# Attention and two gated layers on one core: the first chunk's first group multiplied in float32, its weights and activations split later

## Chip, core and metric

The kernel runs on one core of one Trainium2 chip. The metric is the device time of one execution in microseconds (us). TensorE (PE) multiplies into PSUM banks, VectorE (DVE) and ScalarE (ACT) do the elementwise work, GpSimd (POOL) helps, and SyncE (SP) issues every transfer from one queue, in order.

## What is computed

Three layers stand one behind the other. Attention over 2 x 8 heads, 768 positions and 64 features sees 31 neighbours and one summary (maximum of k, mean of v) of each of 24 blocks of 32 rows; its output is 1536 tokens x 512. A gated layer of width 1536 and a leaky one of width 2048 follow:

```python
x = attention(q, k, v)                     # 1536 x 512, float32
y = (x @ w_a * (x @ w_b)) @ w_out          # moe_*, weights are float64
h = y @ w_in;  out = maximum(0.01 * h, h) @ w2_out   # moe2_*, float64
```

## The kernel before

The tokens are worked in three chunks of 512 (`NC`), the feature axis in pieces of 128. Attention handles one *pair* at a time: two heads and 512 query rows; four pairs make a chunk. A pair runs through k and q transposes (L472, L500), scores (L518), masked minimum and exponential (L531, L535), scaling (L543 to L545), transposes of the probabilities (L553) and the value product (L565). Block sums of v enter through `v_sums` (POOL additions L425, DVE reduction L435), `v_place` (L452) and `put_sums` (POOL copy L196), once for each half of the heads.

The weights come as float64, in 512 KB pieces: `stage` loads one, and `convert` makes a float32 number of its two words in five steps (L332 and L336, L340, L345, L351, L357) and then splits it into a rounded float32r part (`high`, ACT, L362) and what is left (`rest_of`, DVE, L365). The activations are split in the same way (L575 and L576 for x, L603 and L604 for the gated product). A product is three float32r matmuls of 128x512 (`mm3`, L583): part by part, without the product of the two small parts.

The gated layer is worked in three groups (`s`) of `M1` = 4 slices of its width, and in each group chunk by chunk; a unit is a group and a chunk. In a unit four slices give a and b (4 x 2 x 4 products), then the four output tiles of y take 16 more. The first two slices of unit (0, 0) are multiplied during attention of chunk 0, as each x tile comes (`early`). Attention of chunk 1 is interleaved with unit (0, 0), that of chunk 2 with unit (0, 1). A group's 12 converted pieces serve all three chunks, and 14 fit (`W_EARLY`).

Order: the code emits instructions by due times (`attention_ops`), background steps of `convert` go in between (`tick`), and a scheduler then fixes one order for each engine at build time. At run time every engine, and SP's queue, goes strictly in that order and waits for what it needs.

Of the kernel before, what the change touches and what calls it, by code (L numbers as in the profile page):

```python
# [21 lines left out]
def kernel(  # L22
# [43 lines left out]
    M1 = 4  # L66
# [13 lines left out]
    q_p = att.enter_context(tc.tile_pool(name="q", bufs=3))  # L80
# [113 lines left out]
    def put_sums(i, p):  # L194
        for j, b, hp, g, n in runs(p):
            nc.gpsimd.tensor_copy(  # L196
                out=vw_of[i][W : W + NB, :, j * G : (j + n) * G, :],
                in_=vs_t[b, 2 * hp // HV][:, 2 * hp % HV : 2 * hp % HV + 2, :]
                .unsqueeze(2)
                .to_broadcast([NB, 2, n * G, D]),  # L200
            )
# [5 lines left out]
    def attention_ops():  # L207
# [3 lines left out]
        for i, p in enumerate(sum(pairs, [])):  # L211
# [4 lines left out]
            for m, (b, hp) in enumerate(dict.fromkeys(x[:2] for x in p)):  # L216
                vi, r = divmod(2 * hp, HV)
                if (b, hp) not in seen:
                    seen.add((b, hp))
                    add(-18, LOAD, load_k, b, hp)  # L220
                    for j in range(2):
                        add(2 * m + j - 12, PRODUCT, k_prep, b, hp, j)
                    if r == 0:
                        add(-4, LOAD, load_vb, b, vi)
                        add(-4, SIDE, v_sums, b, vi)
                        add(7, PRODUCT, v_place, b, vi)
            add(-14, LOAD, load_q, i, p)
# [15 lines left out]
    for t in vw_t:  # L243
        nc.gpsimd.memset(t, 0.0)
# [4 lines left out]
    ident = const.tile([P, P], F32, tag="ident", name="ident")  # L249
    make_identity(nc, ident)  # L250
    negm = []
    for kind in ("first", "mid", "last"):
        t = const.tile([P, P], F32, tag=f"negm_{kind}", name=f"negm_{kind}")
        nc.gpsimd.memset(t, 0.0)
        nc.gpsimd.memset(t[:, W : W + NB], -math.log(BLK))
        nc.gpsimd.memset(t[:, W + NB : SC], BIG)
        for c in range(2):
            for o, c0, c1 in ((0, 0, W), (W, SC, P)):
                loc = t[c * W : (c + 1) * W, c0:c1]

                nc.gpsimd.affine_select(
                    out=loc, in_=loc, compare_op=ALU.is_ge, fill=BIG,
                    base=o - 1, pattern=[[1, c1 - c0]], channel_multiplier=-1,
                )
                nc.gpsimd.affine_select(
                    out=loc, in_=loc, compare_op=ALU.is_ge, fill=BIG,
                    base=2 * WIN - 1 - o, pattern=[[-1, c1 - c0]], channel_multiplier=1,
                )
        if kind == "first":
            nc.gpsimd.memset(t[:, 0:WIN], BIG)  # L270
        if kind == "last":
            nc.gpsimd.memset(t[:, P - WIN :], BIG)
        negm.append(t)
# [4 lines left out]
    units = [(s, c) for s in range(NF1 // M1) for c in range(NC)]  # L278
    slices2 = [(s * M2 + i, c) for s in range(NF2 // M2) for c in range(NC) for i in range(M2)]
    uses = []  # L280
    for s, c in units:
        fs = range(s * M1, (s + 1) * M1)
        uses += [(nm, f) for f in fs for nm in "ab"] + [("o", f) for f in fs]
# [11 lines left out]
    room = {"early": W_EARLY, "late": 0}  # L295
# [20 lines left out]
    def convert():  # L316
# [8 lines left out]
        home = "early" if room["early"] else "late"  # L325
        assert room[home], key
        room[home] -= 1
        t = {}

        def low():  # L330
            t["r"] = wcv_p.tile([P, 512], I32, tag="wr", name="wr")
# [3 lines left out]
            t["c"] = wcv_p.tile([P, 512], I32, tag="wc", name="wc")  # L335
# [23 lines left out]
        def high():  # L359
            pool = wsp_p if home == "early" else late["wsp"]  # L360
            t["w"] = pool.tile([P, 2, 512], F32R, tag="wsp", name="wsp")
            nc.scalar.copy(out=t["w"][:, 0], in_=t["c"].bitcast(F32))  # L362

        def rest_of():
            nc.vector.tensor_tensor(  # L365
                out=t["w"][:, 1], in0=t["c"].bitcast(F32), in1=t["w"][:, 0].bitcast(F32),
                op=ALU.subtract,
            )
            w_of[key] = t["w"], home

        bg.extend([low, clamp, shift, join, add, high, rest_of])

    def may_convert():
        return cnt["conv"] < len(pieces) and room["early"] + room["late"] > 0

    def tick(n):
        for _ in range(n):
            if not bg and may_convert():
                convert()
# [9 lines left out]
    def weights(key):  # L389
# [443 lines left out]
```

## Time and profile before

| | us |
|---|---|
| median of 3 runs (661.61 to 661.86) | 661.84 |
| profiled execution | 661.53 |
| its span | 659.8 |
| PE busy in the span | 636.2 (96%) |
| DVE, ACT, POOL busy | 418.1, 270.8, 48.5 |
| mean granted PE clock (1 is 2.4 GHz) | 0.992 |

"Busy" counts an instruction from start to end, and matmuls overlap; so where throughput matters, a matmul is priced by the distance from one start to the next in a dense run, and not by its mean duration. The page puts 88% of the chain that ended last on PE. Its slices show where that is not so: PE below 9 tenths only in the first 100 us, and there DVE at 9 tenths and the transfers at 200 GB/s.

### The profile page before, as it was taken

How to read it: one execution, taken by the hardware profiler on the slowest of the kernel's cores; microseconds unless marked ns; L12 is line 12 of the kernel's file. 1: busy time of each engine (PE TensorE's matmuls, PEld its weight loads, DVE VectorE, ACT ScalarE, POOL GpSimd, SP SyncE). 2: the span in 40 equal slices, each digit the busy share in tenths (PEclk: the TensorE clock that was granted, in tenths of full speed). 3: DMA queues.
4: the chain of work that ended last, by engine and by line, in shares of the span. 5: the costliest groups of instructions: out<-in, count | busy, mean ns of one | idle time of the engine just before them, and what ended most of it. 6: DMA issues, size and time to landing. Idle time of an engine off the chain costs nothing.

```text
span 659.8 us, 9339 instructions
## 1 busy us (share of the span) xinstructions
PE 636.2 (96%) x3440; PEld 519.3 (79%) x3440; DVE 418.1 (63%) x952; ACT 270.8 (41%) x609; POOL 48.5 (7%) x79
## 2 busy tenths in 40 slices
PE   5797989999999999999999999999999999999997
PEld 4576767777888888888888888888888888888886
DVE  3999889955999962699623869732279532422323
ACT  3776787653545421344222535322255322222221
POOL 7254042000000000000000000000000000000000
PEclk9898999999999999999999999999999999999999
DMA  8997744512334430244200232400013000100101
GB/s 196 232 224 194 171 106 108 149 25 65 128 129 138 149 96 1 64 129 127 65 0 1 67 93 73 152 1 0 1 56 105 1 0 1 64 1 1 64 1 64
DMA packets 72622, 53.43 MB, mean 81 GB/s; under 512 B 46208, under 2 KB 66688, under 8 KB 72576
## 3 DMA queue, kind: packets, MB, share of 16 engines
q1 hardware_dynamic: 72576, 52.84, 28.0%
q8 instruction: 27, 0.44, 0.3%
q14 instruction: 19, 0.16, 0.1%
HBM read 49.68 MB, written 3.15 MB: 80 GB/s over the span
## 4 chain that ended last, share of the span: by engine, by line
PE 88%; DVE 6%; POOL 2%; DMA 1%; issue 1%; SPq 1%; ACT 0%; POOLq 0%; DVEq 0%
PE ps_t L583 38%; PE ps_c L583 18%; PE ps_a L583 14%; PE ps_b L583 13%; PE ps_t L518 2%; PE ps_t L565 1%; DVE pm L545 1%; PE ps_t L553 1%; DMA vb<-in_v_dram 1%; DVE pm L531 1%; POOL vb L425 1%; PE ps_t L472 1%; SPq L182 1%; DVE sm L543 0%; DVE acc L688 0%
## 5 line engine op out<-in xcount | busy, mean ns | idle before, releaser
L583 PE MATMUL ps_t<-x,wsp 128*128 128x512 f32 x336 | 78.4, 389 | 0.0
L583 PE MATMUL ps_c<-wsp,gs 128*128 128x512 f32 x288 | 75.9, 389 | 0.0
L583 PE MATMUL ps_t<-wsp,gs 128*128 128x512 f32 x288 | 74.7, 389 | 0.0
L583 PEld LDWEIGHTS ps_t<-x,wsp 128*128 128x128 f32 x336 | 63.1, 188 | 13.1
L583 PE MATMUL ps_t<-ys,wsp 128*128 128x512 f32 x288 | 71.9, 389 | 0.0
L583 PE MATMUL ps_a<-x,wsp 128*128 128x512 f32 x252 | 66.0, 399 | 1.8 <-ACT x L575 1.0
L583 PE MATMUL ps_b<-x,wsp 128*128 128x512 f32 x252 | 65.3, 395 | 0.0
L583 PEld LDWEIGHTS ps_t<-wsp,gs 128*128 128x128 f32 x288 | 54.0, 188 | 11.3
L583 PEld LDWEIGHTS ps_c<-wsp,gs 128*128 128x128 f32 x288 | 54.1, 188 | 11.2
L583 PEld LDWEIGHTS ps_t<-ys,wsp 128*128 128x128 f32 x288 | 54.1, 188 | 11.2
L583 PE MATMUL ps_c<-gs,wsp 128*128 128x512 f32 x240 | 61.0, 394 | 0.0
L336 ACT ACTIVATE wc<-wst 128x512 f32<-128x512 f32 x68 | 45.7, 674 | 28.9 <-DVE wsp L365 28.8
L362 ACT CAST wsp<-wc 128x512 fp32r<-128x512 f32 x68 | 42.1, 622 | 34.4 <-DVE wc L357 27.5
L583 PEld LDWEIGHTS ps_a<-x,wsp 128*128 128x128 f32 x252 | 46.8, 190 | 11.9 <-ACT x L575 1.3
L790 DVE SCALAR_TENSOR_TENSOR h<-h,ps_t 128x512 f32<-128x512 f32 x24 | 16.5, 686 | 60.3 <-ACT h L789 60.3
L583 PEld LDWEIGHTS ps_b<-x,wsp 128*128 128x128 f32 x252 | 46.6, 189 | 9.5 <-issue 0.3
L365 DVE TENSOR_TENSOR wsp<-wc,wsp 128x512 fp32r<-128x512 f32 x68 | 46.9, 693 | 8.5 <-ACT wsp L362 8.5
L583 PEld LDWEIGHTS ps_c<-gs,wsp 128*128 128x128 f32 x240 | 44.4, 188 | 9.6 <-DVE wr L332 0.2
L357 DVE CUSTOM_DVE_ANT_0 wc<-wc,wr 128x1024 uint16<-128x1024 uint16 x68 | 48.8, 718 | 0.5
L604 DVE TENSOR_TENSOR gs<-h,gs 128x512 fp32r<-128x512 f32 x48 | 33.1, 690 | 22.8 <-ACT gs L603 22.7
L583 PE MATMUL ps_t<-gs,wsp 128*128 128x512 f32 x192 | 47.5, 389 | 0.0
L351 DVE SCALAR_TENSOR_TENSOR wc<-wst,wc 128x512 int32<-128x512 int32 x68 | 46.6, 688 | 0.3
(94 smaller groups left out, 863.5 us busy)
## 6 DMA issues: line engine op xcount, KB each, us to landing
wst<-in_moe_w_out_dram SPq DMA_DIRECT2D x28, 512.0 KB, 3.3
wst<-in_moe_w_in_dram SPq DMA_DIRECT2D x16, 512.0 KB, 3.7
wst<-in_moe_w_a_dram SPq DMA_DIRECT2D x12, 512.0 KB, 4.4
wst<-in_moe_w_b_dram SPq DMA_DIRECT2D x12, 512.0 KB, 3.7
k<-in_k_dram SPq DMA_DIRECT2D x16, 192.0 KB, 3.6
vb<-in_v_dram SPq DMA_DIRECT2D x8, 384.0 KB, 5.4
out_dram<-acc SPq DMA_DIRECT2D x12, 256.0 KB, 2.0
q<-in_q_dram SPq DMA_DIRECT2D x16, 128.0 KB, 2.9
```

The lines of the kernel that those rows point to most:

```text
L182: nc.sync.dma_start(out=t[p0 : p0 + o1 - o0, c, w0:w1, :], in_=src)
L336: nc.scalar.activation(out=t["c"].bitcast(F32), in_=hi_w.bitcast(F32), func=AF.Abs)
L351: nc.vector.scalar_tensor_tensor(out=t["c"], in0=hi_w, scalar=-0x40000000, in1=t["c"], op0=ALU.bitwise_and, op1=ALU.bitwise_or,)
L357: nc.vector.tensor_tensor(out=t["c"], in0=t["c"], in1=t["r"], op=ALU.add)
L362: nc.scalar.copy(out=t["w"][:, 0], in_=t["c"].bitcast(F32))
L365: nc.vector.tensor_tensor(out=t["w"][:, 1], in0=t["c"].bitcast(F32), in1=t["w"][:, 0].bitcast(F32), op=ALU.subtract,)
L425: nc.gpsimd.tensor_tensor(out=a, in0=a, in1=b, op=ALU.add)
L472: nc.tensor.transpose(ps[:, i * P : (i + 1) * P], k2[:, g * (GT // P) + i].rearrange("p c d -> p (c d)"), ident)
L518: nc.tensor.matmul(out=ps[h, w, :], lhsT=qt[h, w * W : (w + 1) * W], rhs=kts[h, (g * G + w) * SC : (g * G + w) * SC + P], start=True, stop ...
L583: nc.tensor.matmul(out=ps, lhsT=w(a), rhs=x(b), start=first and j == 0, stop=last and j == 2)
L604: nc.vector.tensor_tensor(out=t[:, 1], in0=src, in1=t[:, 0].bitcast(F32), op=ALU.subtract)
L790: nc.vector.scalar_tensor_tensor(out=h, in0=h, scalar=0.01, in1=ps, op0=ALU.mult, op1=ALU.max)
```

## The change

For chunk 0 of group 0 alone, products are single float32 matmuls of whole weights and whole activations (`kt_mm0`, and in `y_products`), 48 in number. `convert` stops after five steps for the first 12 pieces; `next_work` splits these when all 12 are converted, followed by the four x tiles of chunk 0 (`split_x0`). The gated product of unit (0, 0) isn't split. The block sums of v are made once for all heads of a batch, from tiles of half blocks, by DVE alone; the sums of two half blocks are joined by a constant matrix `place` in `v_place`. The k summaries are copied by DVE in place of POOL, two of three masks are DVE copies of the first, and the pools for staged weights and q hold two tiles in place of three.

```diff
-    M1 = 4
+    M1 = (4, 4, 4)
-    wst_p = ctx.enter_context(tc.tile_pool(name="wst", bufs=3))
+    wst_p = ctx.enter_context(tc.tile_pool(name="wst", bufs=2))
-    wsp_p = ctx.enter_context(tc.tile_pool(name="wsp", bufs=W_EARLY))
+    wsp_p = ctx.enter_context(tc.tile_pool(name="wsp", bufs=2 * W_EARLY))
...
-                        add(-4, LOAD, load_vb, b, vi)
-                        add(-4, SIDE, v_sums, b, vi)
+                        add(-5, LOAD, load_vb, b)
+                        add(-4, SIDE, v_sums, b)
...
+    whole = pieces[: 3 * M1[0]]
...
-        bg.extend([low, clamp, shift, join, add, high, rest_of])
+        bg.extend([low, clamp, shift, join, add])
+        if key not in whole:
+            bg.extend(split(key, lambda: t["c"], home))
+
+    def next_work():
+        if cnt["conv"] < len(whole) or not to_split:
+            convert()
+            return
+        key = to_split.pop(0)
+        room["early"] -= 2
+        bg.extend(split(key, lambda: w_whole[key], "early"))
+        if len(to_split) == len(whole) - X_SPLIT:
+            bg.extend(x0_split)
...
-        def add(a, b):
-            nc.gpsimd.tensor_tensor(out=a, in0=a, in1=b, op=ALU.add)
+            lambda i=i, d=d: nc.vector.tensor_reduce(
+                out=v0[:, i, d : d + D // 2],
+                in_=vb_tiles[i][:, :, d : d + D // 2].rearrange("p j d -> p d j"),
...
-            nc.gpsimd.tensor_copy(
+            nc.vector.tensor_copy(
                 out=kts[:, 0:NW, W : W + NB],
...
+            if c == 0:
+                raw.append(g_p.tile([P, 2, T], F32, tag="gs", name="raw", bufs=max(M1)))
+                nc.scalar.copy(out=raw[hp][:, 0], in_=src)
+                x0_split.extend(split_x0(hp))
+                continue
...
+    def kt_mm0(ps, w, kt):
+        nc.tensor.matmul(
+            out=ps, lhsT=w[:, kt * P : (kt + 1) * P], rhs=raw[kt][:, 0],
+            start=kt == 0, stop=kt == KT - 1,
+        )
...
+            if first:
+                nc.tensor.matmul(
+                    out=ps, lhsT=ws[i][:, e * P : (e + 1) * P], rhs=raw[i][:, 1],
+                    start=i == 0, stop=i == n - 1,
+                )
+                return
...
-        pace["bg"] = {(0, 0): 4, (0, 1): 1, (0, 2): 3}.get((s, c), 1.3)
+        first = (s, c) == (0, 0)
+        pace["bg"] = {(0, 0): 6, (0, 1): 0.5, (0, 2): 3}.get((s, c), 1.3)
```

Three places show what moves. On DVE, where the first two weight pieces are finished, before (L365 is the split of a piece, L576 that of an x tile, L357 the last step of a conversion):

```order
L351 SCALAR_TENSOR_TENSOR wc<-wst,wc 128x512
L545 TENSOR_TENSOR pm<-pm,sm 128x512
L543 TENSOR_SCALAR sm<-sm 128x4
L365 TENSOR_TENSOR wsp<-wc,wsp 128x512
L357 ISA wc<-wc,wr 128x1024
L576 TENSOR_TENSOR x_0_524<-ps_t_507,x_0_524 128x512
L544 RECIPROCAL sm<-sm 128x4
L482 TENSOR_REDUCE ks_98<-ps_t_464 128x16
```

The same place of the change (L395 is L351 there, L401 is L357, L601 is L545):

```order
L395 SCALAR_TENSOR_TENSOR wsp<-wst,wsp 128x512
L600 RECIPROCAL sm<-sm 128x4
L599 TENSOR_SCALAR sm<-sm 128x4
L401 ISA wsp<-wsp,wr 128x1024
L601 TENSOR_TENSOR pm<-pm,sm 128x512
L600 RECIPROCAL sm<-sm 128x4
L538 TENSOR_REDUCE ks_98<-ps_t_425 128x16
L538 TENSOR_REDUCE ks_98<-ps_t_475 128x8
L601 TENSOR_TENSOR pm<-pm,sm 128x512
L545 COPY kts_94<-ks_98 128x12x24
```

Both splits are gone from here, and a copy of k summaries has come in. All 12 weight splits and the four x splits (L319, L652) now stand together, far later, where attention of chunk 2 begins.

On PE, where products of chunk 1 (x_0 to x_3 with number 1110 and above) and y products of unit (0, 0) (ps_c) meet, before:

```order
L583 MATMUL ps_a<-x_2_1268,wsp 128x512
L583 MATMUL ps_b<-x_2_1268,wsp 128x512
L553 MATMUL ps_t_1690<-ident,pm 128x128 x4
L583 MATMUL ps_c_1594<-gs,wsp 128x512 x2
L583 MATMUL ps_c_1595<-gs,wsp 128x512 x2
```

and in the change (L805 is a y product of unit (0, 0), L662 a float32r product, x_0_1000 chunk 1):

```order
L805 MATMUL ps_c_1441<-raw,wsp 128x512
L805 MATMUL ps_c_1442<-raw,wsp 128x512
L609 MATMUL ps_t_1308<-ident,pm 128x128 x4
L662 MATMUL ps_a<-x_0_1000,wsp 128x512 x2
L805 MATMUL ps_c_1441<-raw,wsp 128x512
L805 MATMUL ps_c_1442<-raw,wsp 128x512
```

Before, the y products follow the first products of chunk 1; in the change 6 of the 16 come ahead of these, and each is one row instead of three.

On SP, from the third q load on, before and then the change:

```order
L310 DMA wst<-in_moe_w_a_dram 128x4x256
L310 DMA wst<-in_moe_w_b_dram 128x4x256
L310 DMA wst<-in_moe_w_a_dram 128x4x256
L133 DMA k<-in_k_dram 128x6x64 x2
```

```order
L351 DMA wst<-in_moe_w_a_dram 128x4x256
L351 DMA wst<-in_moe_w_b_dram 128x4x256
L132 DMA k<-in_k_dram 128x6x64 x2
L177 DMA vw_100<-in_v_dram 48x64 x2
```

Two pieces are loaded ahead now and not three, and the third follows only behind both batches' v tiles and the k tiles of the fifth head pair.

## Rows read from the trace of the kernel before

**Rows 1.** By stretch: length, busy PE, PEld, DVE, ACT, POOL; clock, DMA share, GB/s.

```profile
0.00:20.50 20.50, 11.19 (x84) 9.02 (x86) 9.70 (x42) 9.49 (x34) 13.17 (x50) 0.98 0.89 226
20.50:68.00 47.50, 39.72 (x380) 30.62 (x378) 44.87 (x140) 33.36 (x110) 20.04 (x17) 0.90 0.85 205
68.00:97.10 29.10, 26.21 (x301) 20.81 (x297) 25.22 (x94) 21.86 (x80) 9.02 (x10) 1.00 0.51 123
97.10:656.00 558.90, 558.88 (x2683) 458.85 (x2683) 337.39 (x679) 206.14 (x388) 6.26 (x3) 1.00 0.20 62
```

**Rows 2.** PE matmuls by form up to 97.1 us: count, busy, mean ns, idle before.

```profile
L518 PE MATMUL ps_t<-kts,qt 64*64 64x128 f32 x272 | 21.5, 304 | 2.8 <-ACT pt L555 1.5 <-POOL negm_last L272 1.2
L583 PE MATMUL ps_a<-x,wsp 128*128 128x512 f32 x37 | 12.0, 433 | 1.0 <-ACT x L575 1.0
L565 PE MATMUL ps_t<-pt,vw 128*64 128x64 f32 x224 | 9.9, 234 | 0.7 <-ACT pt L555 0.6
L472 PE MATMUL ps_t<-ident,k 128*128 128x128 f32 x48 | 9.7, 343 | 8.6 <-DMA k<-in_k_dram 4.6 <-DVE ks L482 3.9
L553 PE MATMUL ps_t<-ident,pm 128*128 128x128 f32 x60 | 9.3, 281 | 4.6 <-DVE nb L531 3.1 <-DVE pm L545 1.4
L583 PE MATMUL ps_b<-x,wsp 128*128 128x512 f32 x24 | 7.9, 412 | 0.0
L583 PE MATMUL ps_c<-x,wsp 128*128 128x512 f32 x24 | 7.6, 411 | 0.6 <-ACT wsp L362 0.6
L500 PE MATMUL ps_t<-ident,q 128*128 128x128 f32 x36 | 7.5, 343 | 0.0
L452 PE MATMUL ps_t<-v,ident 96*24 96x64 f32 x32 | 2.5, 221 | 1.0 <-ACT qt L504 0.7 <-DVE v L435 0.3
```

**Rows 3.** Chain of waits, dense runs on PE: start, time until the next piece.

```profile
75.72 1.08 PE ps_t L565 x32
...
79.02 1.02 PE ps_t L518 x16
...
82.97 0.87 PE ps_t L553 x8
83.84 0.56 PE ps_t L452 x8
...
177.40 2.72 PE ps_a L583 x12
```

**Rows 4.** Timeline of DVE: start, duration, instruction.

```profile
34.32 1.64 DVE L357 CUSTOM_DVE_ANT_0 wc<-wc,wr 128x1024 uint16<-128x1024 uint16 x1
...
49.34 0.68 DVE L365 TENSOR_TENSOR wsp<-wc,wsp 128x512 fp32r<-128x512 f32 x1
49.94 0.68 DVE L357 CUSTOM_DVE_ANT_0 wc<-wc,wr 128x1024 uint16<-128x1024 uint16 x1
...
53.73 1.76 DVE L545 TENSOR_TENSOR pm<-pm,sm 128x512 f32<-128x512 f32 x1
...
58.17 1.75 DVE L545 TENSOR_TENSOR pm<-pm,sm 128x512 f32<-128x512 f32 x1
...
63.35 0.69 DVE L545 TENSOR_TENSOR pm<-pm,sm 128x512 f32<-128x512 f32 x1
```

**Rows 5.** Timeline of POOL in the same stretch.

```profile
53.49 3.12 POOL L425 TENSOR_TENSOR vb<-vb,vb 96x512 f32<-96x512 f32 x2 [5.51 <-DMA q<-in_q_dram]
...
57.78 1.59 POOL L425 TENSOR_TENSOR vb<-vb 96x512 f32<-96x512 f32 x1
```

**Rows 6.** DVE reductions of v by form: count, busy, mean ns, idle before.

```profile
L435 DVE TENSOR_REDUCE v<-vb 96x32 f32<-96x256 f32 x8 | 4.5, 589 | 0.3 <-POOL vb L425 0.3
```

**Rows 7.** Timeline of SP's queue: start, time of issue, instruction.

```profile
52.27 0.40 SPq L310 DMA_DIRECT2D wst<-in_moe_w_a_dram  x1
```

**Rows 8.** DMA issues of the page: count, size of one, median us to landing.

```profile
wst<-in_moe_w_a_dram SPq DMA_DIRECT2D x12, 512.0 KB, 4.4
```

**Rows 9.** Timeline of PE: the first scores.

```profile
9.70 1.97 PE L518 MATMUL ps_t<-kts,qt 64*64 64x128 f32 x16 [1.17 <-POOL negm_last L272]
```

More of the change, by code (lines that the diff above doesn't have):

```diff
@@ L278 @@
-    units = [(s, c) for s in range(NF1 // M1) for c in range(NC)]
+    negm = [
+        const.tile([P, P], F32, tag=f"negm_{kind}", name=f"negm_{kind}")
+        for kind in ("first", "mid", "last")
+    ]
+    t = negm[1]
+    nc.gpsimd.memset(t, 0.0)
+    nc.gpsimd.memset(t[:, W : W + NB], -math.log(BLK))
+    nc.gpsimd.memset(t[:, W + NB : SC], BIG)
+    for c in range(2):
+        for o, c0, c1 in ((0, 0, W), (W, SC, P)):
+            loc = t[c * W : (c + 1) * W, c0:c1]
+            nc.gpsimd.affine_select(
+                out=loc, in_=loc, compare_op=ALU.is_ge, fill=BIG,
+                base=o - 1, pattern=[[1, c1 - c0]], channel_multiplier=-1,
+            )
+            nc.gpsimd.affine_select(
+                out=loc, in_=loc, compare_op=ALU.is_ge, fill=BIG,
+                base=2 * WIN - 1 - o, pattern=[[-1, c1 - c0]], channel_multiplier=1,
+            )
@@ L279 @@
+    assert sum(M1) == NF1
+    group1 = [range(sum(M1[:s]), sum(M1[: s + 1])) for s in range(len(M1))]
+    units = [(s, c) for s in range(len(M1)) for c in range(NC)]
     slices2 = [(s * M2 + i, c) for s in range(NF2 // M2) for c in range(NC) for i in range(M2)]
@@ L281 @@
     for s, c in units:
[L282 to L283 removed]
+        uses += [(nm, f) for f in group1[s] for nm in "ab"] + [("o", f) for f in group1[s]]
     behind = []
@@ L294, with half, split, high @@
     staged, w_of = {}, {}
-    room = {"early": W_EARLY, "late": 0}
+    room = {"early": 2 * W_EARLY, "late": 0}
+    whole = pieces[: 3 * M1[0]]
+    w_whole, to_split, used, done0 = {}, list(whole), set(), set()
+    def half(home):
+        pool = wsp_p if home == "early" else late["wsp"]
+        return pool.tile([P, 512], F32R, tag="wsp", name="wsp")
+    def split(key, c, home):
+        t = []
+        def high():
+            t.append(half(home))
+            nc.scalar.copy(out=t[0], in_=c().bitcast(F32))
+        def rest_of():
+            t.append(half(home))
+            nc.vector.tensor_tensor(
+                out=t[1], in0=c().bitcast(F32), in1=t[0].bitcast(F32), op=ALU.subtract
+            )
+            w_of[key] = t, home
+            done0.add(key)
+            whole_done(key)
+        return [high, rest_of]
+    def whole_done(key):
+        if key in w_whole and key in used and key in done0:
+            del w_whole[key]
+            room["early"] += 1
+    def whole_used(key):
+        used.add(key)
+        whole_done(key)
     F_LO = float(np.array([0x38000000], np.uint32).view(np.float32)[0])
@@ L402, in weights, with weights0 @@
         return w
+    def weights0(key):
+        i = use_no["at"]
+        assert uses[i] == key, (uses[i], key)
+        use_no["at"] += 1
+        while key not in w_whole:
+            if not bg:
+                next_work()
+            step()
+        return w_whole[key].bitcast(F32)
     spent = []
@@ L645 @@
             rest.append(o)
-    gs = [b_out(ab0["b", f][1], a_out(ab0["a", f][1])) for f in range(2)]
+    for f in range(2):
+        b_out0(ab0["b", f][1], a_out(ab0["a", f][1]), f)
     later_ops, held = [], []
@@ L741 @@
             cnt["credit"] = 0.0
-        for i in todo:
-            pa = first_product(("a", s * M1 + i), xt, c)
+        for f in todo:
+            pa = first_product(("a", f), src, c)
             g = a_out(pa)
             interleave()
-            pb = first_product(("b", s * M1 + i), xt, c)
-            gs.append(b_out(pb, g))
+            pb = first_product(("b", f), src, c)
+            if first:
+                b_out0(pb, g, f)
+            else:
+                gs.append(b_out(pb, g))
             interleave()
@@ L760 @@
         gs = []
+        if first:
+            for f in group1[0]:
+                whole_used(("o", f))
+            while len(x0_done) < KT:
+                if not bg:
+                    next_work()
+                step()
     acc = []
```

229 lines of the change are left out of this document (115 added, 114 removed).

## Prediction

> **What bounds the kernel now.** I read the stretches first. From 97.1 us on PE is busy all the time at full clock, so there the kernel is a list of matmuls at a fixed pace [rows 1]. Ahead of that it is not: from 20.5 to 68.0 us DVE is busy 44.9 of 47.5 us and the transfers 85% of the time, while PE, at a mean clock of 0.90, has less to do [rows 1]. The question is therefore how much PE time is lost before 97.1 us, and what the change adds to the list.
>
> PE's busy time counts overlapping matmuls twice over, so I price by dense runs [rows 3]: a 128x512 float32r matmul takes 2.72/12 = 0.227 us, a transposition 0.87/8 = 0.11, a record of the scores 1.02/16 = 0.064, of the value product 1.08/32 = 0.034, of `v_place` 0.56/8 = 0.07. Up to 97.1 us PE has done [rows 2] 85 products x 0.227 = 19.3, 272 x 0.064 = 17.3, 224 x 0.034 = 7.6, 144 transpositions x 0.11 = 15.8 and 32 x 0.07 = 2.2: 62.2 us. So 34.9 us are lost by then.
>
> **The price of a float32 product.** No row shows one of 128x512. The attention matmuls are float32, and except for transpositions each stands in the trace as two records (272 for the 136 scores in the order). The smallest price is two records at the float32r pace, 0.45 us. Against it speaks that one float32 transposition of 128 columns takes 0.11 us [rows 3], twice what 0.227 gives for 128 columns. Four such pieces and two records give 0.88; eight pieces of 64 columns as in `v_place` give 8 x 0.07 x 2 = 1.12, in which the fixed part is counted eight times. I take 0.89, near the transposition, against 3 x 0.227 = 0.68 now. The 48 products cost 48 x 0.21 = +10.1 us on PE. The new `v_place` is 20 matmuls for 16: 8 records x 0.07 = +0.6.
>
> The Trainium skill speaks against the change here: "FP8 and Floating Point Precision", TensorE Precision Notes, says that true float32 takes four passes through the array. By it a product is an estimated 4 x 0.227 = 0.91 us and the 48 cost 11.0 us; the rows come within 1 us of it.
>
> **Until 20.5 us: nothing.** The first scores wait for POOL's last mask until 9.70 us [rows 9]. One mask of three and the k summaries on DVE let them start about 1.9 us earlier. DVE pays it back: six reductions of v at about 0.6 (one of half the elements takes 0.59 with its start-up, 0.5 from start to start [rows 6]) for two at 0.5, three k copies and two mask copies at an estimated 0.35 and 0.17, +4.0 us in all, some of it in DVE's own waits. I put the sum at 0, between -2 and +2.
>
> **From 20.5 to 68.0 us, DVE.** The stretch ends with the second multiplication of a and b (L615; in the change the second `b_out0`). A split of 512 columns takes 0.60 us from start to start [rows 4]. Gone from this stretch are 6 weight splits and 4 x splits, 10 x 0.60 = 6.0. Two reductions of v have moved ahead (-1.0), three k copies have come (+1.05). DVE's work falls from 37.9 to 32.0 us by the two orders: -5.9.
>
> Then the stalls. L545 takes 0.69 us, but 1.76 and 1.75 where POOL adds block sums [rows 4, 5]; six instructions of this stretch are stretched in that way beside L425, L357 at 34.3 us first and L545 at 58.2 last, together by 4.7 us. The additions leave POOL, so -4.7. POOL's copies L196 stay.
>
> The Trainium skill has this as a rule: "SBUF — State Buffer", Who interferes with whom, says that a DVE instruction with two SBUF inputs, or a copy in a two-port mode, and a GpSimd instruction that reads SBUF exclude each other. The trace agrees (0.69 against 1.76). By the rule the reductions bring no new stall, but the three k copies may stand behind an L196; with stalls of 1.75 - 0.69 = 1.06 us each that would be up to +3.2, and the forecast would shrink to nothing.
>
> **From 20.5 to 68.0 us, transfers.** 47.5 - 5.9 - 4.7 = 36.9 would end the stretch at 57.4. But the weights come later now. In SP's order the fifth piece (a2) stands behind 11.5 MB in the change; before, 12.0 MB had been queued when the seventh piece was issued at 52.27 us [rows 7], which lands about 4.4 later [rows 8]. In proportion a2 lands at 54 us. DVE comes to it after 23.5 us of its work behind 20.5, at 44, or some 49 with the stalls that stay and the third piece (8.8 MB, 39 us). Behind it stand 8.4 us of work and another piece (b2, 12.3 MB, 57 us). That ends the stretch at 62. If the queue, less stalled, moves data 5% faster, at 59.5. I take 61.0: -7.0 of the 10.6 us.
>
> **From 61 us to the first product of chunk 1.** PE has finished the first two slices about 1.5 us before DVE multiplies them: 59.5. Until chunk 1's first product it has, counted in its order, 22 float32 products (six of them y), and attention: 77.8 us in sum from the start, less 40.3 us until there, 37.5 us. DVE has 32.8 us of work in the same time, with the conversion of the last six pieces, the transfers are ahead of need (o0 behind 15.7 MB, some 74 us, wanted at 78). So PE sets the pace; I allow 2.4 us of waits; from 68.0 to 97.1 PE is now idle for 2.9 us [rows 1]. Chunk 1's first product starts at 99.4 us, 2.3 later than before.
>
> **After it.** Before, 12 float32r matmuls of b3 and 48 of y are left of unit (0, 0), 60 x 0.227 = 13.6 us; in the change 10 y products, 8.9. Four more transpositions are done (-0.4), one product less (+0.2). The list behind is 4.9 us shorter. The 12 weight splits and 4 x splits then come in one block, 16 x 0.60 = 9.6 us on DVE and as many casts on ACT; the 8.9 us of y products and attention of chunk 2 cover them, and by the order the pieces of group 2 are wanted only after another 92 us of PE work. If that cover fails, each missing split costs 0.60.
>
> **Sum.** 2.3 - 4.9 = -2.6 us. From the profiled 661.53 that is 658.9; the median of the runs is 0.3 above it, so 659.2. In other terms: 10.7 us more PE work against 13.3 us less lost time. It breaks even when chunk 1 starts at 102.0.
>
> **Rivals.**
> (1) Slower: two engines in fixed orders, both nearly full. In the stretch from 59.5 us a block of four float32 products (3.6 us) stands ahead of scores for which DVE waits, and DVE's conversions stand ahead of scalings for which PE waits. For it: DVE's share of the old 68.0 to 97.1 us is 87% [rows 1], and such waits stand there already. Against: a float32 product whose weights are there needs nothing from DVE, and fills where attention waits. If a quarter of DVE's 32.8 us can't be overlapped, the waits are 8.2 in place of 2.4, chunk 1 starts at 105.2, and the time is 665.0. It decides from 5.0 us of waits.
> (2) No change: the transfers give nothing, a2 and b2 come as computed and each holds a further in-order wait; the stretch ends at 63.5, and chunk 1 starts at 101.9: 661.7. For it: 85% DMA share, two staged pieces in place of three. Against: the old stretch ran at the same 85%, and DVE was busy 44.9 of 47.5 us all the same [rows 1].
> (3) Larger gain: the transfers keep up, as SP is no longer held by the buffers of the split v tiles; the stretch ends at 57.4, waits are 1.5: 94.9, 7.1 us gained, 654.7.
> (4) The float32 product costs something else: at 1.12 us it adds 7.4 us, 666.6; at 0.45 DVE sets the pace to 95.5 and the list shrinks by a further 4.4, 651.
>
> **How the numbers follow.** Forecast 0.38, (1) 0.22, (2) 0.16, (3) 0.18, (4) 0.06, of which 0.04 is the dear side. Two tenths of a per cent, 1.3 us, is about what a measurement of this kernel can tell from no change. Of the forecast 0.36 lies beyond it: faster 0.36 + 0.18 + 0.02 = 0.56; same 0.02 + 0.16 + 0.02 of (1) = 0.20; slower 0.24. The range goes from somewhat below (3) to somewhat above (1), 653 to 666; the forecast's own is 656.5 to 661.
>
> **What will show it.** In the new profile: float32 products of 0.85 to 0.92 us in a dense run; no DVE instruction over 1.2 us beside POOL between 20 and 60 us, except at L196's times; DVE waiting for a weight transfer near 40 and 50 us; the second `b_out0` near 61 us; the first product of chunk 1 near 99 us; PE full from there, with no wait for a split weight. A chunk 1 later than 102 us, or a float32 product above 1 us, makes the forecast wrong.

## The result: slower, 666.5 us

| | before | changed |
|---|---|---|
| median, us | 661.8 | 666.48 (665.14 to 668.37) |
| ratio to before | 1 | 1.0072, 95% interval 1.0056 to 1.0089 |
| profiled execution, us (span) | 661.53 (659.8) | 666.15 (664.4) |
| first product of chunk 1, us | 97.1 | 107.4 (forecast 99.4) |

The forecast was 659.2. The page of the changed kernel, and its stretches, which answer to [rows 1]:

```profile
span 664.4 us, 9226 instructions
PE 644.2 (97%) x3400; PEld 510.3 (77%) x3400; DVE 420.9 (63%) x964; ACT 268.3 (40%) x607; POOL 20.6 (3%) x38
```

```profile
0.00:20.50 20.50, 11.95 (x84) 9.57 (x85) 12.53 (x49) 8.85 (x32) 5.24 (x22) 1.00 0.83 218
20.50:68.00 47.50, 41.16 (x363) 26.58 (x363) 37.30 (x134) 30.12 (x103) 8.10 (x8) 0.93 0.79 205
68.00:97.10 29.10, 27.61 (x228) 16.36 (x227) 25.62 (x82) 16.06 (x57) 2.83 (x4) 1.00 0.43 117
```

From 20.5 to 68 us DVE is busy 37.3 us where it was 44.9, and POOL 8.1 for 20.0: the relief came. PE is busy for 41.2 us of it, 39.7 before, and the stretch ends only 0.7 us sooner, at 67.4.

What was relieved and what was not stands on DVE's timeline (start, duration; L487 reduces v, L389 and L601 are a conversion step and a scaling, L700 is `b_out0`), and beside it POOL's:

```profile
16.09 3.85 DVE L487 TENSOR_REDUCE v<-vb 128x32 f32<-128x512 f32 x4
19.86 0.16 DVE L599 TENSOR_SCALAR sm<-sm 128x4 f32<-128x4 f32 x1
...
27.31 1.26 DVE L389 TENSOR_SCALAR wsp<-wsp 128x512 int32<-128x512 int32 x1
...
38.01 1.42 DVE L601 TENSOR_TENSOR pm<-pm,sm 128x512 f32<-128x512 f32 x1
...
66.68 0.69 DVE L700 TENSOR_TENSOR raw<-ps_c,g 128x512 f32<-128x512 f32 x1 [1.05 <-ACT g L696]
```

```profile
26.69 1.59 POOL L191 COPY vw<-vs 24x1024 f32<-24x1024 f32 x1 [2.73 <-PE ps_t L621]
37.85 1.03 POOL L191 COPY vw<-vs 24x1024 f32<-24x1024 f32 x1 [9.56 <-PE ps_t L621]
```

The stretched instructions that are left stand beside POOL's copies; those of [rows 4, 5] are gone. But a reduction of v takes 3.77/4 = 0.94 us from start to start, not 0.6, and the second `b_out0` starts at 66.7 and ends at 67.4 us, where 61.0 was forecast. The chain of waits shows what stood before it (start, time until the next piece):

```profile
49.83 0.60 PE ps_t L528 x4
50.43 0.02 issue
50.45 0.39 ACT kts L533
50.84 4.28 DMA wst<-in_moe_w_a_dram
55.12 0.02 issue
55.14 0.43 ACT wsp L380
55.57 3.80 DMA wst<-in_moe_w_b_dram
59.37 0.02 issue
59.40 0.66 ACT wsp L380
60.05 0.48 ACT raw L633
60.53 0.04 issue
60.58 1.73 PE ps_a L670 x2
62.31 1.72 PE ps_b L670 x2
```

The chain puts the flights of two transfers on the path, 8.1 us: pieces a2 and b2, issued at 50.84 and 55.57. Not all of that is waiting. For a2 DVE waits 0.30 us only, since both engines had other work almost until it came. For b2 ACT waits 2.12 us, in its first step of the piece (L380), and next in ACT's order stands the copy of the last x tile (L633), for which PE waits 2.02 us:

```profile
55.14 0.43 DVE L373 TENSOR_SCALAR wr<-wst 128x512 int32<-128x512 uint32 x1 [0.30 <-DMA wst<-in_moe_w_a_dram]
59.40 0.66 ACT L380 ACTIVATE wsp<-wst 128x512 f32<-128x512 f32 x1 [2.12 <-DMA wst<-in_moe_w_b_dram]
60.58 1.73 PE L670 MATMUL ps_a<-raw,wsp 128*128 128x512 f32 x2 [2.02 <-ACT raw L633]
...
65.81 1.04 PE L609 MATMUL ps_t<-ident,pm 128*128 128x128 f32 x8
```

PE waited near this place in the kernel before too, and longer, but for DVE:

```profile
60.58 0.69 PE L472 MATMUL ps_t<-ident,k 128*128 128x128 f32 x2 [3.91 <-DVE ks L482]
```

So one wait was taken away and another, shorter one stands in its place. PE's clock falls behind it (0.57 granted from 60.5 to 64.0 us, shown beside e1 below), which the float32 products pay: the block of four products with the last x tile (the fourth early block) takes 5.2 us, from 60.58 to 65.81, and 1.73 us of that for its first two records, where in a dense run eight take 3.58:

```profile
78.71 3.65 PE L670 MATMUL ps_a<-raw,wsp 128*128 128x512 f32 x8
82.29 1.09 PE L574 MATMUL ps_t<-kts,qt 64*64 64x128 f32 x16
...
107.40 0.71 PE L662 MATMUL ps_a<-x,wsp 128*128 128x512 f32 x2
```

So a float32 product is 3.58/4 = 0.895 us (0.89 forecast). The last line is the first product of chunk 1.

**Work and lost time.** As in the forecast I price the PE records of a stretch by dense runs ([rows 3]; 0.4475 for a float32 record of 128x512) and call the rest of the stretch lost. Up to 97.1 us the changed kernel has 240 score records, 66 float32, 132 transpositions, 192 of the value product and 40 of `v_place`: 68.5 us of work, 28.6 lost; up to 300 us 34.1 lost, before 40.4. Up to the end of the fourth early block the changed kernel has 40.2 us of work and 25.6 lost, the kernel before 37.1 and 30.0: of the 4.4 us saved there, 3.1 went into more work. The products add 48 x (0.895 - 0.68) = 10.3 us and `v_place` 0.6; 6.3 are saved; 10.9 - 6.3 = +4.6, as measured by the spans. (This sum has to come out: lost time is what is left of the same 300 us, and behind them both kernels do the same work on a busy PE. It shows where the time went, and is no test of a cause.) The forecast had 10.7 and 13.3. Where did the other 7.0 us go?

### The profile page after: what moved, and what is told of

Its sections match the earlier page's. It is cut to its first block, busy times and chain, and to the rows that moved or that the text cites. A ratio compares the mean times of both kernels' runs of the same rounds, so it can differ in the third digit from the quotient of the medians.

```text
span 664.4 us, 9226 instructions
## 1 busy us (share of the span) xinstructions
PE 644.2 (97%) x3400; PEld 510.3 (77%) x3400; DVE 420.9 (63%) x964; ACT 268.3 (40%) x607; POOL 20.6 (3%) x38
## 4 chain that ended last, share of the span: by engine, by line
PE 90%; DVE 5%; DMA 2%; issue 1%; SPq 1%; ACT 0%; DVEq 0%
PE ps_t L662 37%; PE ps_c L662 16%; PE ps_a L662 12%; PE ps_b L662 12%; PE ps_t L574 3%; PE ps_c L805 2%; PE ps_t L609 2%; PE ps_t L621 1%; DVE v L487 1%; PE ps_b L670 1%; DMA wst<-in_moe_w_b_dram 1%; DVE pm L587 1%; PE ps_t L556 1%; DMA wst<-in_moe_w_a_dram 1%; DVE ks L538 0%
## 5 line engine op out<-in xcount | busy, mean ns | idle before, releaser
L662 PE MATMUL ps_t<-x,wsp 128*128 128x512 f32 x336 | 78.4, 389 | 0.0
L662 PE MATMUL ps_c<-wsp,gs 128*128 128x512 f32 x288 | 75.5, 389 | 0.0
L662 PE MATMUL ps_t<-wsp,gs 128*128 128x512 f32 x288 | 74.9, 389 | 0.0
L662 PEld LDWEIGHTS ps_t<-x,wsp 128*128 128x128 f32 x336 | 63.1, 188 | 13.1
L662 PE MATMUL ps_t<-ys,wsp 128*128 128x512 f32 x288 | 71.9, 389 | 0.0
L662 PEld LDWEIGHTS ps_t<-wsp,gs 128*128 128x128 f32 x288 | 54.1, 188 | 11.2
L662 PEld LDWEIGHTS ps_c<-wsp,gs 128*128 128x128 f32 x288 | 54.1, 188 | 11.2
L662 PEld LDWEIGHTS ps_t<-ys,wsp 128*128 128x128 f32 x288 | 54.1, 188 | 11.2
L380 ACT ACTIVATE wc<-wst 128x512 f32<-128x512 f32 x56 | 37.9, 676 | 51.6 <-DVE wsp L319 13.6
L662 PE MATMUL ps_a<-x,wsp 128*128 128x512 f32 x216 | 54.6, 395 | 0.0
L662 PE MATMUL ps_b<-x,wsp 128*128 128x512 f32 x216 | 54.2, 393 | 0.0
L315 ACT CAST wsp<-wc 128x512 fp32r<-128x512 f32 x56 | 34.8, 621 | 39.5 <-DVE wc L401 17.2
L319 DVE TENSOR_TENSOR wsp<-wc,wsp 128x512 fp32r<-128x512 f32 x56 | 38.4, 686 | 16.1 <-ACT wsp L315 15.4
L662 PE MATMUL ps_c<-gs,wsp 128*128 128x512 f32 x192 | 47.8, 390 | 0.0
L662 PE MATMUL ps_t<-gs,wsp 128*128 128x512 f32 x192 | 47.4, 389 | 0.0
L662 PEld LDWEIGHTS ps_a<-x,wsp 128*128 128x128 f32 x216 | 40.1, 188 | 9.0 <-issue 0.6
L662 PEld LDWEIGHTS ps_b<-x,wsp 128*128 128x128 f32 x216 | 40.1, 188 | 8.5 <-issue 0.3
L591 ACT ACTIVATE pm<-pm,nb 128x128 f32<-128x128 f32 x96 | 37.5, 393 | 20.0 <-DVE nb L587 20.0
L688 ACT CAST gs<-h 128x512 fp32r<-128x512 f32 x48 | 29.8, 621 | 32.0 <-DVE h L907 32.0
L662 PEld LDWEIGHTS ps_t<-gs,wsp 128*128 128x128 f32 x192 | 36.0, 188 | 7.5
```

What stands on the lines that cost most here:

```text
L315: nc.scalar.copy(out=t[0], in_=c().bitcast(F32))
L319: nc.vector.tensor_tensor(out=t[1], in0=c().bitcast(F32), in1=t[0].bitcast(F32), op=ALU.subtract)
L380: nc.scalar.activation(out=t["c"].bitcast(F32), in_=hi_w.bitcast(F32), func=AF.Abs)
L591: nc.scalar.activation(out=pm[:, w, :], in_=pm[:, w, :], func=AF.Exp, scale=-1.0, bias=nb[:, w : w + 1], accum_out=sm[:, w : w + 1],)
L662: nc.tensor.matmul(out=ps, lhsT=w(a), rhs=x(b), start=first and j == 0, stop=last and j == 2)
L688: nc.scalar.copy(out=t[:, 0], in_=src)
```

## Experiments

Three theories stand in the expectations. T: the staged transfers set the end of the stretch. V: the reductions of v cost more than priced. F: the float32 products cost through waits in fixed orders, not through their work.

The median of the kernel before moved between 661.5 and 662.5 us from one measurement to the next, so a version is judged by its ratio to the before that was measured beside it; where a median is set against an expected range, up to 0.7 us of this drift is in it. One per cent is 6.6 us. "Lost" is lost PE time up to 300 us, from the one profiled execution; that of e3 is 2.9 us longer than e3's median, those of e4 and e14 1.2 shorter and 1.2 longer, the others within 1 us.

| run | what | ratio, 95% interval | lost, us |
|---|---|---|---|
| before | | 1 | 40.4 |
| changed | | 1.0072 (1.0056 to 1.0089) | 34.1 |
| e1 | changed, three staged | 1.0029 (1.0014 to 1.0044) | 32.0 |
| e2 | before, two staged | 1.0040 (1.0026 to 1.0055) | 44.1 |
| e3 | changed, v as before | 1.0118 (1.0094 to 1.0143) | 41.9 |
| e4 | before, v changed | 1.0024 (1.0010 to 1.0038) | 41.0 |
| e5 | changed, half reductions | 1.0019 (0.9999 to 1.0040) | 32.0 |
| e6 | e1 and e5 | 1.0008 (0.9988 to 1.0029) | 30.7 |
| e7 | e1, float32 for 16 products | 1.0078 (1.0054 to 1.0101) | 44.6 |
| e8 | before, set-up changed | 0.9988 (0.9969 to 1.0006) | 40.0 |
| e9 | e1, v summed by PE | 1.0162 (1.0142 to 1.0183) | 33.2 |
| e10 | e1, v summed by additions | 1.0170 (1.0151 to 1.0189) | 42.5 |
| e11 | e8, v summed by PE | 1.0086 (1.0069 to 1.0103) | 37.6 |
| e12 | e8, v summed by additions | 0.9947 (0.9927 to 0.9967) | 36.2 |
| e13 | e10 in 6 steps | 1.0062 (1.0040 to 1.0083) | 34.8 |
| e14 | e12 in 6 steps | 0.9991 (0.9974 to 1.0008) | 41.0 |
| e15 | e13, weights early | 1.0065 (1.0042 to 1.0088) | 33.9 |
| e16 | e14, weights early | 0.9928 (0.9902 to 0.9955) | 35.6 |
| e17 | e8 with the products | 1.0231 (1.0201 to 1.0261) | 45.7 |
| e18 | e12, weights early | 0.9960 (0.9943 to 0.9977) | 36.9 |

**The staging buffer (e1, e2).** The first in the changed kernel, the second in the one before:

```diff
-    wst_p = ctx.enter_context(tc.tile_pool(name="wst", bufs=2))
+    wst_p = ctx.enter_context(tc.tile_pool(name="wst", bufs=3))
```

```diff
-    wst_p = ctx.enter_context(tc.tile_pool(name="wst", bufs=3))
+    wst_p = ctx.enter_context(tc.tile_pool(name="wst", bufs=2))
```

> The changed kernel with three staging buffers for raw weight pieces in place of its two; nothing else. Theory T (transfers): with two buffers the fifth and sixth piece (a2, b2) are issued only at 50.8 and 55.6 us, ScalarE's first conversion step waits for them in order, and the raw copy of the fourth x tile stands behind it; with three they are issued at some 42 and 48 us, the fourth early block ends at 59 to 62 us instead of 65.8, the second b_out0 at 60 to 63 instead of 67.3, the first product of chunk 1 comes at 101 to 104 instead of 107.4, and the time is 660 to 663 us. Theory F (float32 products ahead of scores on PE, in-order waits): the waits only change places, and the time stays within 1.3 us of 666.5. Theory V (reductions of v on VectorE twice as long as estimated): also within 1.3 us of 666.5.

> The kernel before with two staging buffers instead of three; nothing else. Theory T: the same buffer costs the kernel before too, since its fifth piece then can't be issued at 36.4 us: its stretch ends 2 to 4 us later than 68.0, and the time is 663.5 to 666. Rival: before was held by VectorE (44.9 of 47.5 us busy), and a later transfer hides behind that: within 1.3 us of 661.8.

The buffer is worth 0.43% in the one and 0.40% in the other, some 2.7 us, more than half of the loss of 0.72%. In e1 a2 and b2 are issued at 38.9 and 41.8 us, PE waits 0.45 us for the last x tile, and its clock stays: the fourth block takes 3.5 us, from 59.64 to 63.18, in place of 5.2. SP, then PE of e1, then the stretch behind that wait in the changed kernel and in e1:

```profile
38.87 0.40 SPq L351 DMA_DIRECT2D wst<-in_moe_w_a_dram  x1
41.84 1.31 SPq L351 DMA_DIRECT2D wst<-in_moe_w_b_dram  x1
```

```profile
59.64 1.13 PE L670 MATMUL ps_a<-raw,wsp 128*128 128x512 f32 x2 [0.45 <-ACT raw L633]
...
63.18 0.60 PE L609 MATMUL ps_t<-ident,pm 128*128 128x128 f32 x4
...
104.89 0.71 PE L662 MATMUL ps_a<-x,wsp 128*128 128x512 f32 x2
```

```profile
60.50:64.00 3.50, 3.42 (x5) 1.50 (x6) 3.03 (x8) 1.50 (x6) 0.00 (x0) 0.57 0.64 170
```

```profile
60.50:64.00 3.50, 3.50 (x17) 1.74 (x17) 2.24 (x6) 2.29 (x7) 0.00 (x0) 1.00 0.82 231
```

Theory T holds in kind and not in size: the fourth block ends 2.6 us sooner, 0.9 by its start and 1.7 by its length, and chunk 1 comes 2.5 us sooner, but the block's end (63.2), chunk 1 (104.9) and the time (664.0) all lie above T's ranges. V and F, which had no change, are refuted for this part. Chunk 1 is still 5.5 us behind the forecast. e2's 665.1 us is in T's range.

**The v part (e3, e4).** In e3 `load_vb`, `v_sums` and `v_place` of before go back into the changed kernel; e4 puts the changed ones into the kernel before.

```diff
-                        add(-5, LOAD, load_vb, b)
-                        add(-4, SIDE, v_sums, b)
+                        add(-4, LOAD, load_vb, b, vi)
+                        add(-4, SIDE, v_sums, b, vi)
...
```

```diff
-                        add(-4, LOAD, load_vb, b, vi)
-                        add(-4, SIDE, v_sums, b, vi)
+                        add(-5, LOAD, load_vb, b)
+                        add(-4, SIDE, v_sums, b)
...
```

> The changed kernel with the v part put back: block sums by half the heads, added on GpSimd and reduced on VectorE, loads of v in two halves, v_place as before; the rest (float32 products, late splits, masks, two staging buffers) stays. Theory V: the six reductions of 0.95 us ahead of the first scores' scalings and six more at 74 to 80 us cost more than the stalls they removed; without them 662 to 664 us. Theory T: only half a batch of v (0.75 MB less) stands ahead of the weights, so weights come some 3 us earlier, but the stalls beside GpSimd's additions return (4.7 us): 665 to 668. Prediction as it stood: the stalls return on VectorE, slower by 4 us, 669 to 671.

> The kernel before with only the v part of the change: whole batches of v in half blocks, twelve reductions on VectorE, no additions on GpSimd, the new v_place; its q tiles have two buffers and the rounding tile one, to make room. Theory V: slower, 664 to 667, as VectorE is the busy engine there and the reductions are twice as long as estimated (6 x 0.35 us more in each batch). Theory T: the weights wait behind 0.75 MB more of v: 663 to 665. Prediction as it stood: stalls of 4.7 us go, v costs about 1 us, the stretch ends 3 us earlier: 658 to 660.

The two disagree: beside float32 products the new v part is worth 0.5%, beside float32r products it costs 0.2% (there together with one q tile and one rounding tile fewer). e3's 670.5 us is in the range of the forecast's own reasoning, e4's 664.0 in that of T and at the edge of V's; no theory had both. A reading that no run tests: what the part saves in stalls it spends on reductions, and which of the two shows depends on whether DVE or the order sets the pace.

**Half the reductions (e5, e6),** without and with the third buffer:

```diff
-                in_=vb_tiles[i][:, :, d : d + D // 2].rearrange("p j d -> p d j"),
+                in_=vb_tiles[i][:, : BLK // 4, d : d + D // 2].rearrange("p j d -> p d j"),
```

> The changed kernel with each reduction of v over 8 of the 16 positions of a half block (it leaves out the sums of the other 8), so that one takes some 0.5 us instead of 0.95, as the forecast had priced it; two staging buffers. Theory V: 2.7 us less on VectorE before 20 us, the first float32 block comes 1 to 2 us earlier than 28.6, and the time falls by 1 to 2.5 us to 664 to 665.5. Theory T (the staged transfers set the end of the stretch): it starts earlier and waits longer for a2 and b2: within 1 us of 666.5, fourth block's end still at 65 to 66 us.

> The changed kernel with three staging buffers and the half reductions of e5 (it leaves out the sums of half the positions of v). Theories T and V together: what the reductions cost shows once the transfers are ahead, 661 to 662.8 against 664.0 with three buffers alone. Theory F (in-order waits around float32 blocks hold the stretch): no further gain, 663.3 to 664.7.

At the size that the forecast had priced, the reductions give back 0.5% without the buffer (3.5 us by the ratios, more than V's 1 to 2.5) and 0.2% with it, which the intervals can't tell from nothing. V is confirmed in sign by e5 alone, and not for the place where it looked. e5 has lost 2.1 us less up to 20.5 us, but then PE waits 2.45 us for the copy behind b2, and the fourth block ends at 65.4 in place of 65.8, as T had it. The other 1.5 of the 1.9 us between the two profiled spans (664.4 and 662.5) come from the second batch of v: in the changed kernel PE waits for DVE behind the reductions of 74 to 80 us, and in e5 that wait is gone. e5, then the changed kernel:

```profile
60.24 2.08 PE L670 MATMUL ps_a<-raw,wsp 128*128 128x512 f32 x2 [2.45 <-ACT raw L633]
...
65.42 1.04 PE L609 MATMUL ps_t<-ident,pm 128*128 128x128 f32 x8
```

```profile
85.73 0.66 PE L609 MATMUL ps_t<-ident,pm 128*128 128x128 f32 x4 [1.49 <-DVE x L638]
```

Both corrections together still leave e6 at before, not 0.4% below it.

**Fewer float32 products (e7).** Only the early ones; the rest of the edit puts back the splits of x and the float32r products that belong to this line:

```diff
-    whole = pieces[: 3 * M1[0]]
+    whole = pieces[:4]
...
```

> The changed kernel with three staging buffers, in which only the first two slices of chunk 0 (16 of the 48 products) are in float32; their four weights are split later as in the change, but x tiles are split as they come, and the other 32 products of chunk 0 are three float32r matmuls again. PE then has 16 x 0.215 = 3.4 us more work than before instead of 10.3. Theory of the sum (time before 97 us is work plus lost PE time): if the lost time stays at the 25.5 us of the three-buffer kernel, 661.8 + 3.4 - 8.9 = 656 us; if the splits that come back (four of x, four of w_out among them) hold VectorE as they did before, half of the lost time returns and it is 660 to 661. Theory F in its strong form (float32 blocks cost through waits, not work): 663 or more.

At 668.9 us it is above both sums, since 44.6 us are lost. Theory F's 663 or more holds by the number, but the longest wait behind 68 us is no float32 block's: the splits are back there, and PE waits for one:

```profile
83.59 4.14 PE L660 MATMUL ps_a<-x,wsp 128*128 128x512 f32 x10 [2.64 <-DVE wsp L319]
```

This one wait is 2.6 of 12.6 us more lost than in e1. Its pacing was set for the full change, so it says that bringing the splits forward again costs waits, and not what a tuned hybrid would take.

**The set-up (e8).**

```diff
-            nc.gpsimd.tensor_copy(
+            nc.vector.tensor_copy(
                 out=kts[:, 0:NW, W : W + NB],
...
```

> The kernel before with only the set-up part: the identity first, one mask on GpSimd and two copied on VectorE, and the k summaries copied on VectorE; v and products as before. The forecast had: first scores 1.9 us earlier, and three k copies (some 0.3 us each) more on a busy VectorE. If the early start carries through, 660 to 661; if VectorE takes it back, 661.2 to 662.4.

No difference that can be told: DVE has the first scores at 9.6 us instead of 11.8 (PE starts them at 9.70 in [rows 9], and takes 1.97), and the gain is gone by the end.

**Other sums of v (e9 to e12).** Six float32 matmuls with a table of 1/32 (e9, e11), or a tree of additions on DVE (e10, e12); e9 and e10 on e1, e11 and e12 on e8.

```diff
+                lhsT=place[:, c0 : c0 + NB],
+                rhs=vb_tiles[i // 2].rearrange("p (n h) d -> p n h d", n=2)[:, i % 2].rearrange("p h d -> p (h d)"),
...
```

```diff
+                ops.append(lambda t=t, n=n, out=out: nc.vector.tensor_tensor(
+                    out=out, in0=t[:, 0:n], in1=t[:, n : 2 * n], op=ALU.add))
```

> The changed kernel with three staging buffers and the block sums of v made on TensorE: v comes as 128 positions by 512 columns, and six float32 matmuls with a 1/32 table of 24 columns give the sums of a batch directly, in place of six reductions of 0.95 us on VectorE and 20 small matmuls. Theory V: VectorE has 5.7 us less ahead of 20.5 us and 5.7 less at 74 to 80 us; the 4.1 us more on TensorE lie in lost time for the first batch, and count in full for the second: 660.5 to 663 against 664.0. If the reductions hid no more than they cost: 664 to 667.

> The changed kernel with three staging buffers and the half blocks of v added in a tree of contiguous VectorE additions (512, 256, 128 and 64 elements, an estimated 0.60 + 0.33 + 0.20 + 0.15 us for each of three tiles, 3.9 us a batch) in place of strided reductions (5.7 us a batch). Theory V: 1.8 us less before 20.5 us, 662.5 to 663.7. Theory T: no difference from three buffers alone, 663.6 to 664.6.

> The kernel before with the set-up part and the sums of v on TensorE as in e9 (the rounding tile has one buffer to make room); all products stay float32r. VectorE then loses its reductions (4 us in all) and the stalls beside GpSimd's additions (4.7 us) in a stretch where it is the busy engine; TensorE gets 4.3 us more in each batch, the first in lost time. If the stalls were the price of the kernel before: 656 to 659.5. If, as e4 hinted, relieving VectorE of them gives nothing: 661.5 to 664.

> The kernel before with the set-up part and the sums of v by the additions of e10 on VectorE (q tiles have two buffers, the rounding tile one). VectorE: 3.9 us a batch for 2 and the stalls of 4.7 us; start 1.9 us earlier: 658.5 to 661 if the stalls count, 661.5 to 664 if not.

On PE the sums lose in both, beyond every range expected (673.3 and 668.2 us): they stand ahead of scores for 7.9 us in e9, at 18.5 us, when nothing else may pass. The tree gives e12, 0.5% faster than before (658.7 us, in the range for stalls that count), and e10, 1.7% slower, which nobody expected. In e10 DVE waits for a weight:

```profile
45.49 0.43 DVE L373 TENSOR_SCALAR wr<-wst 128x512 int32<-128x512 uint32 x1 [5.83 <-DMA wst<-in_moe_w_b_dram]
```

Its fourth piece is issued at 40.7 us, e1's at 35.6. The code takes two background steps behind each product, and 12 additions are 12 steps.

**The same work in six steps, with and without float32 (e13, e14),** on e10 and on e12:

```diff
+            ops += [lambda i=i: adds(i, (8,)), lambda i=i: adds(i, (4, 2, 1))]
```

> The additions of e10 grouped into six background steps a batch (one of 512 elements, one of 256, 128 and 64, for each of three tiles), as many as the reductions were; three staging buffers; the rest as changed. If e10 lost through the count of steps (its fourth weight issued at 40.7 us instead of 35.5, VectorE waiting 5.8 us for it), this one issues it near 35 and takes 661.5 to 663.5. If e10 lost through the additions themselves: above 668.

> e12 with the additions in six steps a batch; products float32r. Same as e12 within 2 us: 657 to 661. Against e13 it has the same set-up, sums of v and staging, and differs in the products and their splits alone. Theory of the sum: the float32 products add 10.7 us of TensorE work and take back 6 to 8.5 of lost time, so e13 is 2 to 4.5 us above this kernel. If the float32 products paid for themselves once v is cheap: e13 is equal or below.

e13 is 1.1% below e10 with the same additions, and issues the fourth piece at 34.4: the count of steps was the cause, though 667.1 misses the 661.5 to 663.5 expected. e14 is 0.4% above e12 by the same edit: there fewer steps cost, and why is not shown. e14's 661.6 is just above its range too. The pair differs in the products and their splits, and with them in the due times of the k and q steps and in the pace of the background steps: 0.7%, 3.9 us by the spans (665.0 and 661.1), 5.5 by the medians. Work and lost time give 10.3 - (41.0 - 34.8) = 4.1. The stretch from 20.5 us on, e13 and then e14:

```profile
20.50:68.00 47.50, 40.51 (x342) 25.74 (x341) 34.06 (x129) 30.54 (x103) 7.69 (x8) 0.89 0.81 220
```

```profile
20.50:68.00 47.50, 38.13 (x352) 28.77 (x353) 40.85 (x134) 31.79 (x108) 7.75 (x8) 0.89 0.74 201
```

DVE has 6.8 us less to do in e13, and its second `b_out0` comes at 67.7 us where e14 has 68.5.

**First weights ahead of v (e15, e16),** on e13 and e14:

```diff
+            if i == 0:
+                add(-6, LOAD, stage)
+                add(-6, LOAD, stage)
```

> e13 with the first two raw weight pieces staged ahead of the first batch of v (on SyncE's queue as its fourth and fifth instruction group, some 13 us earlier). Theory T: VectorE's wait of some 2 us for w_a near 21.6 us goes, and the queue has the same bytes: 0.5 to 2.5 us below e13. Rival: v lands some 4 us later instead, its sums and so the first value product and the first float32 block come later: equal or 1 to 3 us above e13.

> e14 with the first two raw weight pieces staged ahead of the first batch of v. Theory T: 0.5 to 2 us below e14. Rival as for e15: equal or above.

With float32 products nothing happens, as the rival had it. Without them it is the best version, 0.7% faster than before (657.7 us), and the gain on e14 is 3.9 us, twice what theory T had. The pair is 1.4% apart: 8.7 us by the spans, 10.3 - (35.6 - 33.9) = 8.6 by the sum. The same stretch of e15, then e16:

```profile
20.50:68.00 47.50, 42.24 (x378) 27.32 (x380) 35.25 (x130) 29.18 (x102) 7.07 (x8) 0.89 0.82 212
```

```profile
20.50:68.00 47.50, 42.63 (x411) 32.96 (x411) 45.09 (x158) 36.83 (x124) 7.05 (x8) 0.96 0.80 211
```

e16 finishes 411 matmul records in it where before had 380. The granted clock is 0.96 in it, against 0.89 in e15 and in both of e13 and e14: an estimated (0.96 - 0.89) x 47.5 = 3.3 us of PE time, so a good part of what this pair is further apart than the last one stands in the clock, and no run shows whether the products are the reason.

**Products alone (e17), and the steps once more (e18).** e17 is e3 with the third buffer, e18 is e16 with 12 steps:

```diff
-    wst_p = ctx.enter_context(tc.tile_pool(name="wst", bufs=2))
+    wst_p = ctx.enter_context(tc.tile_pool(name="wst", bufs=3))
```

```diff
-            ops += [lambda i=i: adds(i, (8,)), lambda i=i: adds(i, (4, 2, 1))]
+                ops.append(lambda t=t, n=n, out=out: nc.vector.tensor_tensor(
```

> Set-up and float32 products with the sums of v as before (on GpSimd) and three staging buffers: against e8 it differs in the products, their late splits, the rounding tile and the q tiles. Theory of the sum: 10.1 us more TensorE work and 2 to 6 us less lost time than e8: 4 to 8 us above e8, 666 to 670. If the third buffer were the whole cause of e3's 670.5: 663 or less.

> e16 with the additions of v in twelve background steps a batch as in e12. If what set e12 apart from e14 (0.44%) adds to the early transfers, 654 to 656.5; if both only move the same weights forward in the order, 656.5 to 659.

e17 is 2.4% above e8, at 677.5 us far above its range; beside the products the pair differs in the buffers of the rounding and q tiles, and in due times and pace as the others do. Spans are 16.0 us apart, by the sum 10.3 + (45.7 - 40.0) = 16.0. Here DVE waits for POOL's additions:

```profile
36.02 1.07 DVE L495 TENSOR_REDUCE v<-vb 96x32 f32<-96x256 f32 x2 [3.72 <-POOL vb L485]
```

The third buffer makes it worse than e3, so its 2.7 us belong to e1 and e2 and are no constant. e18 (659.6 us) misses its ranges; its ratio is not below that of e12 or e16, so the steps and the early weights do not add.

## Why the prediction was wrong

- **The price of the product** was right: 0.895 us for 0.89. The Trainium skill's four passes ("FP8 and Floating Point Precision", TensorE Precision Notes) gave an estimated 0.91, and the trace agrees with that too.
- **Until 20.5 us** the sum of 0 was right (13.7 us lost before and after), but of wrong parts: a reduction is 0.94 us and not 0.6. I had read it from one of 256 elements [rows 6] and added too little for twice as many. Six of them ate the 2.0 us of the earlier scores.
- **The failed step is "From 20.5 to 68.0 us, transfers": I took 61.0 us for the stretch's end, with PE done with the first two slices at 59.5; it was 67.4 and 65.8.** PE's work up to there was 40.2 us, as forecast; 25.6 were lost and not 19.2. DVE's work in the stretch fell by 7.6 of the 10.6 us forecast. The transfers of a2 and b2 ended at 55.1 and 59.4, near the 54 and 57 computed (the same proportion gives 58 for b2, and 42 and not 39 for the third piece), so the bytes were right. What I left out is the order behind b2: I counted DVE's 8.4 us behind a2, and no wait of another engine for b2. From b2's end to the stretch's end 8.0 us pass. 1.2 of them go by until ACT has done its step for b2 and, behind it, the copy of the last x tile. 5.2 go to PE's block, which comes out of 2.0 us of idleness at a granted clock of 0.57 (mostly the 1.2 GHz level); after 0.45 us of idleness in e1 it has 1.00 and takes 3.5. 1.6 go to ACT and DVE. The third buffer (e1) ends the block 2.6 us sooner, the reductions at their forecast size (e5) 0.4, both together (e6, 63.3 us) 2.5. The other 3.9 of the 6.4 us I can't assign to one wait, and their cause stays open: e10 against e13 shows that the count of background steps alone moves the kernel by 7 us.
- **From there to chunk 1** 41.6 us for 39.9: the work as forecast (37.6 for 37.5), 4.0 lost for 2.4, of which 1.5 are the wait for DVE behind the second batch of reductions.
- **The list behind** and the late splits were right: 5.7 us shorter for 4.9 (107.4 - 97.1 less 4.6), and from 97.1 to 300 us PE is busy 202.8 of 202.9.
- **The rivals.** (1) had the nearest numbers (665.0; chunk 1 at 105.2), but not for its reason: from the fourth block to chunk 1 only 4.0 us are lost, not 8.2. The place was that of (2), though the in-order wait is b2's alone, at more than its price. I gave the two 0.38 together; the range to 666 missed by 0.5 us.
- The Trainium skill's rule on GpSimd and DVE ("SBUF — State Buffer", Who interferes with whom), which counts `tensor_scalar` with `copy` among the instructions that can take both ports, agrees with the trace: the longest stalls left, 1.26 us of a `tensor_scalar` and 1.42 of a scaling with two inputs from SBUF, lie beside POOL's copies.

What the pairs settle is the sign, for kernels paced as these are. At the price of the dense run the products are 10.3 us of work; what they buy back by the spans is 6.2, 1.7 and -5.7 us. In no pair did the float32 products pay. Each pair also changes the due times of the k and q steps and the pace of the background steps; no run changes those alone, so a schedule under which the products pay is not excluded.

## What to carry to other kernels

Count work put on the engine that sets the end at its full price; the waits that it removes elsewhere are worth only what the fixed orders let through (here 6.3 of 13.3 us), so credit them wait by wait and not by busy time. Before counting on a relieved engine, look at the instruction ahead of the critical one on every in-order queue, the helper's too, and at how many buffers feed it. Test such a change by pairs that differ in one part; a step more or less in a paced order moved this kernel by up to 1.1%.

## Not expected of the hardware

A reduction with a stride of 64 elements takes 0.589 us for 256 elements [rows 6] and 1.03 for 512, 1.72 ns an element. Contiguous additions in e13 (count, busy, mean ns):

```profile
L491 DVE TENSOR_TENSOR vb<-vb 128x512 f32<-128x512 f32 x3 | 2.0, 685 | 0.0
L491 DVE TENSOR_TENSOR vb<-vb 128x256 f32<-128x256 f32 x3 | 1.2, 419 | 0.0
```

are 266 ns for 256 elements more, 1.04 ns an element. The Trainium skill ("SBUF — State Buffer", Door 1, on cachelines) says that each access which crosses to another line of 16 bytes pays; a stride of 256 bytes does so each time, and the two rates agree with it. No run changes the stride alone; nearest is a reduction of neighbouring elements in the changed kernel, of k in PSUM, 0.68 us for 512 elements in place of 1.03:

```profile
51.74 0.68 DVE L538 TENSOR_REDUCE ks<-ps_t 128x16 f32<-128x512 f32 x1
```
